# Feed-forward reordered around the first output sums, with the weight sums one place on and half of the next inputs split by GpSimd

## The chip, the cores and the metric

One program runs on one core of a Trainium2 chip. The metric is the device time of one execution in microseconds (us). A profiled execution gives the trace from which the rows below come; times in it count from the first instruction. The engines are named as the profile names them: PE (TensorE, matmuls), PEld (its weight loads), DVE (VectorE), ACT (ScalarE), POOL (GpSimd) and SP (the queue that issues DMAs). Each works through its own instructions strictly in the order in which the program lists them.

## What is computed

Attention with a mix of the heads before and after the softmax, then two feed-forward layers over 1792 tokens of width 768:

```python
x = attention(q, k, v, w_pre, w_post)          # 4 batches, 12 heads, 448 positions, head width 64
h = x @ w_in                                   # 768 -> 2048, layer 0
x = (h * np.cos(h)) @ w_out                    # 2048 -> 768
g, val = x @ w_gate, x @ w_val                 # 768 -> 1536 each, layer 1
out = (g / (1 + np.exp(-g)) * val) @ w_out2    # 1536 -> 768
```

## The kernel before

Attention runs first as a software pipeline. Its steps (`premix`, `rowmax`, `expo`, ...) are entered in a plan by block number; within a block the kinds of step are issued in the order of the table `ORDER`. The first weights of the feed-forward are prepared in attention's last blocks, as kinds of the same table (`w_max`, `w_sum`, `w_sum_all`, `w_unit`, `w_shift`, `w_bits`, `w_split`).

The feed-forward is written out by hand in `steps()`. It runs over pieces (layer, g, t): g is a group of 256 hidden units (8 groups in layer 0, 6 in layer 1), t one of four tiles of 448 tokens. Iteration i works on two pieces at once: the first matmuls and the nonlinearity of piece i, and the second matmuls of piece i-1.

- `l1` makes the hidden values of one half e (128 units): 18 matmuls (L718 to L720) into the PSUM tile `ph`, since each product is made of high and low halves of both operands. In layer 1 there are two columns (gate and value), so 36.
- `hidden` turns `ph` into `gh` (high half) and `gl` (low half). In layer 0: DVE makes `k` (L735) and `r` (L736), ACT takes the sine (L737), DVE multiplies (L739), ACT casts `gh` (L747), POOL subtracts for `gl` (L748). In layer 1: ACT does Silu (L745), DVE multiplies (L746), then the same.
- `l2` makes the six output sums m = 0 to 5 of the piece before, 6 matmuls each (L763 to L765), into the PSUM tile `py`, which has three buffers. Sum m is added to `acc` by DVE (L769), or, in the first group of a layer, copied there by ACT (L767). So the first matmul of the fourth sum (m = 3) must wait until the first sum has been taken out of its buffer, the fifth for the second, the sixth for the third.

Weights are converted between these steps. `fill(n)` issues the next n small steps of a list: one DVE instruction on a slab of weights (L514 maxima, L561, L563, L567 the bits), with the ACT and POOL instructions that belong to it (L553, L591, L592). When the maxima of a batch are complete, `sum_up` puts a tiny matmul `su` (L533) on PE, which spreads the maxima over the partitions, and two DVE instructions that read it (L541, L542); until then the batch's conversion is held back. The same matmul for activations is `sx` (L790, in `next_unit`). `su` and `sx` share one PSUM bank.

Between the layers the outputs of layer 0 become layer 1's inputs X[t], six parts m for each t, each split in a high and a low half: `next_hi` (ACT, L798) with `next_lo` (DVE, L812), or, for t = 0, `next_both` (ACT twice, L805 and L806, and POOL, L807). In the last group of layer 0 each sum's addition is followed by a maximum (L773).

The order inside one iteration before: fill; for each half e: three parts of the next inputs' high halves, `l1`, the whole of `hidden` (with one fill before its last multiply in layer 0), for e = 0 another fill, three parts of the low halves, `sum_up`; then the six sums of `l2`, with fills behind m = 1 and 3 (and 5 in layer 1 and the first iterations), then `sum_up`.

## Time and profile before

| | |
|---|---|
| three runs | 1433.23 us median (1430.79 to 1433.38) |
| the profiled execution, its own time | 1432.4 us |
| its span, first to last instruction | 1430.6 us |
| PE busy | 1393.1 us, 97% of the span |
| DVE busy | 1017.0 us, 71% |
| ACT busy | 615.7 us, 43% |
| POOL busy | 459.3 us, 32% |
| mean granted TensorE clock | 0.996 of full speed |
| DMA | 126.16 MB, mean 88 GB/s |

Matmuls are pipelined and one counts as busy until its end, so PE's busy share says little about small waits; they are read from the starts of the matmuls and from the view of waits. Attention fills the span to about 440 us and thins out until 465 us; layer 0 runs from there to about 960 us, layer 1 to the end.

### The profile page before, as it was taken

Reading aid. Unit: us, or ns where it says so; the run is one execution under the profiler, and the core shown is the slowest. Engines: PE = TensorE matmul, PEld = TensorE weight load, DVE = VectorE, ACT = ScalarE, POOL = GpSimd, SP = SyncE. Lnnn points to the kernel's source line nnn. Section 1 sums busy time; section 2 is a strip of 40 time slices with the busy share of each in tenths; the row PEclk is TensorE's granted clock in tenths of the full one; section 3 lists DMA queues with packets and bytes.
Section 4 is the critical chain, followed back from the end, with each engine's and each line's share of the span. In section 5 each row is a group of like instructions: output and inputs, shape, how many; then the busy total and the mean of one; then the engine's idle time right before and its main releaser. Section 6 shows DMA issues by size and latency. Waiting matters only on the chain.

```text
span 1430.6 us, 25097 instructions
## 1 busy us (share of the span) xinstructions
PE 1393.1 (97%) x9562; PEld 963.6 (67%) x9562; DVE 1017.0 (71%) x2166; ACT 615.7 (43%) x1310; POOL 459.3 (32%) x490
## 2 busy tenths in 40 slices
PE   6899999999999999999999999989999999999998
PEld 3577777767766666767676767656666666666666
DVE  5877887877888668888888888775456566565523
ACT  4676777677665543333333332544422222222210
POOL 2354453453323333333232332322222223222310
PEclk9999999999999999999999999999999999999999
DMA  5554554554556122221221121021211212120012
GB/s 178 148 154 126 162 156 124 157 159 129 150 157 211 55 56 67 67 67 55 58 76 56 56 78 45 23 66 45 67 45 45 67 53 81 45 66 24 1 43 112
DMA packets 100209, 126.16 MB, mean 88 GB/s; under 512 B 29592, under 2 KB 88440, under 8 KB 100088
## 3 DMA queue, kind: packets, MB, share of 16 engines
q1 hardware_dynamic: 99248, 123.26, 29.0%
q8 instruction: 75, 1.23, 0.4%
q10 hardware_dynamic: 840, 1.29, 0.3%
q14 instruction: 46, 0.38, 0.1%
HBM read 75.45 MB, written 10.37 MB: 60 GB/s over the span
## 4 chain that ended last, share of the span: by engine, by line
PE 78%; DVE 16%; ACT 3%; issue 2%; DMA 1%; POOL 0%; ACTq 0%; SPq 0%; DVEq 0%; POOLq 0%
PE ph L718 11%; PE ph L720 10%; PE ph L719 10%; PE psm L232 9%; PE py L763 8%; PE py L764 7%; PE py L765 7%; PE psv L306 5%; PE pss L207 4%; PE psa L281 2%; PE psa L282 2%; PE psa L283 2%; DVE r L736 2%; DVE acc L769 2%; DVE r L739 2%
## 5 line engine op out<-in xcount | busy, mean ns | idle before, releaser
L718 PE MATMUL ph<-x,h_i 128*128 128x448 f16 x960 | 338.9, 353 | 0.0
L719 PE MATMUL ph<-x,h_i 128*128 128x448 f16 x960 | 338.3, 352 | 0.0
L720 PE MATMUL ph<-x,l_i 128*128 128x448 f16 x960 | 338.3, 352 | 0.0
L763 PE MATMUL py<-gh,h_o 128*128 128x448 f32 x672 | 256.9, 382 | 12.8 <-ACT acc L767 6.3
L748 POOL TENSOR_TENSOR gl<-r,gh 128x448 fp32r<-128x448 f32 x112 | 131.8, 1177 | 404.8 <-ACT gh L747 395.8
L764 PE MATMUL py<-gl,h_o 128*128 128x448 f32 x672 | 244.6, 364 | 0.0
L765 PE MATMUL py<-gh,l_o 128*128 128x448 f32 x672 | 244.0, 363 | 0.0
L769 DVE TENSOR_TENSOR acc<-py,acc 128x448 f32<-128x448 f32 x288 | 174.3, 619 | 64.1 <-PE py L765 60.3
L261 POOL TENSOR_SCALAR eh<-e,sm 120x448 f16<-120x448 f32 x180 | 121.5, 675 | 247.5 <-DVE sm L256 160.3
L232 PE MATMUL psm<-x,wpre_sb 120*120 120x448 f32 x360 | 179.3, 581 | 5.6 <-ACT e L245 5.6
L718 PEld LDWEIGHTS <-h_i 128*128 128x128 f16 x960 | 93.8, 98 | 92.6 <-issue 10.3
L720 PEld LDWEIGHTS <-l_i 128*128 128x128 f16 x960 | 93.9, 98 | 87.7 <-POOL l_i L592 0.2
L245 ACT ACTIVATE e<-psm,sm 120x448 f32<-120x448 f32 x180 | 114.8, 638 | 87.5 <-DVE sm L237 79.6
L763 PEld LDWEIGHTS py<-gh,h_o 128*128 128x128 f32 x672 | 126.7, 188 | 38.3 <-DVE acc L769 15.9
L719 PEld LDWEIGHTS <-h_i 128*128 128x128 f16 x960 | 94.1, 98 | 82.2 <-issue 0.3
L237 DVE TENSOR_REDUCE sm<-psm 120x1 f32<-120x448 f32 x180 | 111.0, 617 | 40.3 <-PE psm L232 40.2
L746 DVE SCALAR_TENSOR_TENSOR r<-ph,by_i,r 128x448 f32<-128x448 f32 x48 | 32.8, 684 | 146.5 <-PE ph L720 117.8
L268 DVE SCALAR_TENSOR_TENSOR el<-e,sm,eh 120x448 f16<-120x448 f32 x180 | 136.1, 756 | 0.0
L592 POOL TENSOR_TENSOR l_i<-f_i,h_i 128x384 f16<-128x384 f32 x80 | 81.4, 1018 | 165.2 <-ACT h_i L591 165.1
L765 PEld LDWEIGHTS py<-gh,l_o 128*128 128x128 f32 x672 | 126.5, 188 | 9.0
L764 PEld LDWEIGHTS py<-gl,h_o 128*128 128x128 f32 x672 | 126.8, 189 | 7.4
L747 ACT CAST gh<-r 128x448 fp32r<-128x448 f32 x112 | 63.5, 567 | 155.6 <-DVE r L746 117.8
(103 smaller groups left out, 2284.8 us busy)
## 6 DMA issues: line engine op xcount, KB each, us to landing
r_o<-in_w_out SPq DMA_DIRECT2D x56, 384.0 KB
x<-s SPq DMA_DIRECT2D x84, 210.0 KB
r_i<-in_w_in SPq DMA_DIRECT2D x32, 384.0 KB
x<-s SPq DMA_DIRECT2D x48, 192.5 KB
r_i<-in_w_gate SPq DMA_DIRECT2D x24, 384.0 KB
r_i<-in_w_val SPq DMA_DIRECT2D x24, 384.0 KB
x<-s SPq DMA_DIRECT2D x48, 175.0 KB
qr<-in_qT SPq DMA_DIRECT2D x15, 360.0 KB
```

The costliest lines, as they stand in the source:

```text
L232: nc.tensor.matmul(ps[:120, :S], wpre_sb, X[b, c][:120, k], start=True, stop=True)
L245: nc.scalar.activation(e, PM.pop((b, c, k))[:120, :S], AF.Exp, bias=sm[:, 0:1], scale=1.0, accum_out=sm[:, 1:2])
L261: nc.gpsimd.tensor_scalar(eh, E[b, c, k], sm[:, 3:4], 1.0, op0=ALU.mult, op1=ALU.mult)
L268: nc.vector.scalar_tensor_tensor(el, E.pop((b, c, k)), sm[:, 3:4], eh, op0=ALU.mult, op1=ALU.subtract)
L718: nc.tensor.matmul(ps, wh, xh, start=(kk == 0), stop=False)
L719: nc.tensor.matmul(ps, wh, xl, start=False, stop=False)
L720: nc.tensor.matmul(ps, wl, xh, start=False, stop=(kk == 5))
L748: nc.gpsimd.tensor_tensor(gl, r, f(gh), op=ALU.subtract)
L763: nc.tensor.matmul(ps, wh, gh[:, e], start=(e == 0), stop=False)
L764: nc.tensor.matmul(ps, wh, gl[:, e], start=False, stop=False)
L765: nc.tensor.matmul(ps, wl, gh[:, e], start=False, stop=(e == 1))
L769: nc.vector.tensor_tensor(acc, ps, acc, op=ALU.add)
```

## The change

`hidden` is cut in two: `hidden_a` ends with the sine or the Silu, `hidden_b` holds the multiply, the cast and the subtraction. For the half e = 1, `hidden_b` is issued behind the first output sum (m = 0) with one fill ahead of it, no longer ahead of all six. The second `sum_up` of an iteration goes there too, and a `su` is issued one place later (tick - 2). The next inputs' parts 0 to 2 are issued behind the first half's `hidden_b`, parts 3 to 5 behind the sums m = 1 to 3; parts 3 to 5 of every t (not only of t = 0) are now split by ACT, ACT and POOL, where DVE made the low half. In layer 1's first two groups the scale factors (`w_by`) are made ahead of the fill. In `ORDER`, `w_sum_all`, `w_unit` and `w_shift` stand behind `premix`.

```diff
--- before.py
+++ after.py
@@ -36,8 +36,8 @@
 AT_DVE = (2, 5, 8)
 ORDER = (
     "scale_v", "mixed_out", "l1_part", "norm_hi", "dma_v", "spread", "post", "rowmax", "w_sum",
-    "w_sum_all", "w_unit", "w_bits", "hidden", "norm_lo", "den", "w_max", "w_shift", "w_split",
-    "expo", "lo_q", "dma_q", "lo_k", "qk", "rec", "premix", "pv_out", "hi_k", "dma_k", "w_dma",
+    "w_bits", "hidden", "norm_lo", "den", "w_max", "w_split", "expo", "lo_q", "dma_q", "lo_k", "qk",
+    "rec", "premix", "w_sum_all", "w_unit", "w_shift", "pv_out", "hi_k", "dma_k", "w_dma",
     "x_load", "load_next", "new_scale", "max_v", "pv", "hi_q",
 )
 SM = 1.0 / 8.0
@@ -666,7 +666,7 @@
     def sum_up(self, all=False):
 
         self.tick += not all
-        while self.sums and (all or self.sums[0][-1] < self.tick - 1):
+        while self.sums and (all or self.sums[0][-1] < self.tick - 2):
             *batch, _ = self.sums.pop(0)
             self.w_sum_all(batch)
             self.w_unit(batch)
@@ -719,31 +719,36 @@
         nc.tensor.matmul(ps, wh, xl, start=False, stop=False)
         nc.tensor.matmul(ps, wl, xh, start=False, stop=(kk == 5))
 
-    def hidden(self, layer, g, t, e, fill=0):
+    def hidden(self, layer, g, t, e):
+        self.hidden_a(layer, g, t, e)
+        self.hidden_b(layer, g, t, e)
+
+    def hidden_a(self, layer, g, t, e):
 
         nc = self.tc.nc
         if e == 0:
             self.G[g, t] = tuple(
                 self.p_g.tile([128, 2, S], F32R, tag=f"g{p}", name=f"g{p}{layer}_{g}_{t}") for p in "hl"
             )
-        gh, gl = (x[:, e] for x in self.G[g, t])
         r = self.p_t.tile([128, S], F32, tag="t", name=f"r{layer}_{g}_{t}_{e}")
+        self.part["r", t, e] = r
         if layer == 0:
             ps = self.PH[e, 0]
-            by, turn = (self.by[0, "i", 0, 2 * g + e][:, i, t:t + 1] for i in range(2))
+            turn = self.by[0, "i", 0, 2 * g + e][:, 1, t:t + 1]
             k = self.p_t.tile([128, S], I32, tag="t", name=f"k_{g}_{t}_{e}")
             nc.vector.tensor_scalar(k, ps, turn, 0.25, op0=ALU.mult, op1=ALU.add)
             nc.vector.scalar_tensor_tensor(r, ps, turn, k, op0=ALU.mult, op1=ALU.subtract)
             nc.scalar.activation(r, r, AF.Sin, bias=self.hpi, scale=TWOPI)
-            self.fill(fill)
-            nc.vector.scalar_tensor_tensor(r, ps, by, r, op0=ALU.mult, op1=ALU.mult)
         else:
-            if g < 2:
-                for col in range(2):
-                    self.w_by((1, "i", col, 2 * g + e), t)
-            by = [self.by[1, "i", col, 2 * g + e][:, 0, t:t + 1] for col in range(2)]
-            nc.scalar.activation(r, self.PH[e, 0], AF.Silu, scale=by[0])
-            nc.vector.scalar_tensor_tensor(r, self.PH[e, 1], by[1], r, op0=ALU.mult, op1=ALU.mult)
+            by = self.by[1, "i", 0, 2 * g + e][:, 0, t:t + 1]
+            nc.scalar.activation(r, self.PH[e, 0], AF.Silu, scale=by)
+
+    def hidden_b(self, layer, g, t, e):
+        nc = self.tc.nc
+        gh, gl = (x[:, e] for x in self.G[g, t])
+        r = self.part.pop(("r", t, e))
+        by = self.by[layer, "i", layer, 2 * g + e][:, 0, t:t + 1]
+        nc.vector.scalar_tensor_tensor(r, self.PH[e, layer], by, r, op0=ALU.mult, op1=ALU.mult)
         nc.scalar.copy(gh, r)
         nc.gpsimd.tensor_tensor(gl, r, f(gh), op=ALU.subtract)
 
@@ -793,25 +798,19 @@
         nc.vector.tensor_scalar(self.unit[1][:, t:t + 1], u, 2.0 ** -14, None, op0=ALU.mult)
         nc.vector.reciprocal(by, self.unit[1][:, t:t + 1])
 
-    def next_hi(self, t, ms):
-        for m in range(6)[ms]:
-            self.tc.nc.scalar.activation(self.X[t][0][:, m], self.acc[t][:, m], AF.Copy, scale=self.mx[t][:, 7:8])
-
...
+    def next_part(self, t, m):
+
+        nc = self.tc.nc
+        hi, lo = (x[:, m] for x in self.X[t])
+        by = self.mx[t][:, 7:8]
+        if t == 0 or m > 2:
             x = self.p_acc.tile([128, S], F32, tag="nx", bufs=2, name=f"nx_{t}_{m}")
-            nc.scalar.activation(x, self.acc[t][:, m], AF.Copy, scale=self.mx[t][:, 7:8])
+            nc.scalar.activation(x, self.acc[t][:, m], AF.Copy, scale=by)
             nc.scalar.copy(hi, x)
             nc.gpsimd.tensor_tensor(lo, x, hi, op=ALU.subtract)
-
...
+        else:
+            nc.scalar.activation(hi, self.acc[t][:, m], AF.Copy, scale=by)
+            nc.vector.scalar_tensor_tensor(lo, self.acc[t][:, m], by, hi, op0=ALU.mult, op1=ALU.subtract)
 
     def early_plan(self, s):
 
@@ -858,40 +857,51 @@
             self.now = i
             t_max = i - done - 2
             t_new = t_max - 1
+            L0, g0, t0 = seq[i - 1]
             if i > 1 and i < len(seq):
                 L, g, t = seq[i]
                 for batch in range(1 + L) if t == 0 else ():
                     self.need(("i", L, g, batch))
+                if L and g < 2:
+                    for e in range(2):
+                        for col in range(2):
+                            self.w_by((1, "i", col, 2 * g + e), t)
                 self.fill((3 + (i < 4), 5)[L])
                 shorten = 0 <= t_new < 4
-                for e in range(2):
-                    if shorten:
-                        (self.next_hi if t_new else self.next_both)(t_new, slice(3 * e, 3 * e + 3))
-                    if (i, e) != (2, 0):
-                        self.l1(L, g, t, e)
-                    self.hidden(L, g, t, e, 1)
-                    if e == 0:
-                        self.fill((1, 5)[L])
-                    if shorten and t_new:
-                        self.next_lo(t_new, slice(3 * e, 3 * e + 3))
-                    self.sum_up()
-            L, g, t = seq[i - 1]
-            if t == 0:
-                self.need(("o", L, g))
+                if i != 2:
+                    self.l1(L, g, t, 0)
+                self.hidden_a(L, g, t, 0)
+                self.fill(1)
+                self.hidden_b(L, g, t, 0)
+                self.fill((1, 5)[L])
+                if shorten:
+                    for m in range(3):
+                        self.next_part(t_new, m)
+                self.sum_up()
+                self.l1(L, g, t, 1)
+                self.hidden_a(L, g, t, 1)
+            if t0 == 0:
+                self.need(("o", L0, g0))
             if 0 <= t_max < 4:
                 self.next_max(t_max)
             if i == 1:
                 self.l1(0, 0, 2, 0)
             for m in range(6):
-                self.l2(L, g, t, m)
+                self.l2(L0, g0, t0, m)
                 if i == 1 and m == 0:
                     self.hidden(0, 0, 1, 1)
-                if m in (1, 3) or i == 1 or (m == 5 and (L or i < 4)):
+                if m == 0 and 1 < i < len(seq):
+                    self.fill(1)
+                    self.hidden_b(L, g, t, 1)
+                    self.sum_up()
+                if m in (1, 3) or i == 1 or (m == 5 and (L0 or i < 4)):
                     self.fill(1)
                 if 0 <= t_max < 4 and m == 3:
                     self.next_unit(t_max)
+                if 0 < m < 4 and 0 <= t_new < 4:
+                    self.next_part(t_new, m + 2)
             self.sum_up()
-            del self.G[g, t]
+            del self.G[g0, t0]
         assert not self.todo
```

DVE in layer 0, iteration of piece (0, 4, 1), around the start of the six sums of piece (0, 4, 0); `k` and `r0` belong to the half e = 1, `acc_01<-py0_4_0_m` takes out sum m. Before:

```order
L735 TENSOR_SCALAR k_4_1_1_9942<-ph0_4_1_1_0_9922,by_0_i_0_9_0_9442 128x448
L736 SCALAR_TENSOR_TENSOR r0_4_1_1_9941<-ph0_4_1_1_0_9922,by_0_i_0_9_0_9442,k_4_1_1_9942 128x448
L567 SCALAR_TENSOR_TENSOR f_0_i_0_11_1_9879<-r_0_i_0_11_1_9486,f_0_i_0_11_1_9879 128x384
L739 SCALAR_TENSOR_TENSOR r0_4_1_1_9941<-ph0_4_1_1_0_9922,by_0_i_0_9_0_9442,r0_4_1_1_9941 128x448
L769 TENSOR_TENSOR acc_01_7797<-py0_4_0_0_9954,acc_01_7797 128x448
L769 TENSOR_TENSOR acc_01_7797<-py0_4_0_1_9962,acc_01_7797 128x448
```

and with the change, where L774 is the addition and L751 the multiply:

```order
L739 TENSOR_SCALAR k_4_1_1_9947<-ph0_4_1_1_0_9927,by_0_i_0_9_0_9431 128x448
L740 SCALAR_TENSOR_TENSOR r0_4_1_1_9946<-ph0_4_1_1_0_9927,by_0_i_0_9_0_9431,k_4_1_1_9947 128x448
L774 TENSOR_TENSOR acc_01_7797<-py0_4_0_0_9951,acc_01_7797 128x448
L514 TENSOR_REDUCE u_0_i_0_12_0_9959<-r_0_i_0_12_0_9788 128x1
L751 SCALAR_TENSOR_TENSOR r0_4_1_1_9946<-ph0_4_1_1_0_9927,by_0_i_0_9_0_9431,r0_4_1_1_9946 128x448
L774 TENSOR_TENSOR acc_01_7797<-py0_4_0_1_9964,acc_01_7797 128x448
```

The first sum is taken out right behind `r0`; the fill and the multiply stand between the first and the second sum.

DVE again, between the layers, around the sums of piece (0, 7, 3); `x_12` are the low halves of X[1], `f_1_o` weights. Before:

```order
L812 SCALAR_TENSOR_TENSOR x_12_7213<-acc_01_7797,mx_1_11662,x_12_7213 128x448 x3
L602 TENSOR_SCALAR by_1_i_0_1_0_11986<-unit1_72,u_1_i_0_1_0_11330 128x1
L602 TENSOR_SCALAR by_1_i_1_1_0_11988<-unit1_72,u_1_i_0_1_0_11330 128x1
L746 SCALAR_TENSOR_TENSOR r1_0_0_1_11985<-ph1_0_0_1_1_11966,by_1_i_1_1_0_11988,r1_0_0_1_11985 128x448
L812 SCALAR_TENSOR_TENSOR x_12_7213<-acc_01_7797,mx_1_11662,x_12_7213 128x448 x3
L541 TENSOR_SCALAR u_1_i_0_2_0_11857<-su_1_i_0_2_0_11997 128x2
L542 TENSOR_SCALAR u_1_i_0_2_0_11857<-u_1_i_0_2_0_11857 128x2
L783 TENSOR_REDUCE mx_2_11804<-mx_2_11804 128x1
L769 TENSOR_TENSOR acc_3_7799<-py0_7_3_0_12002,acc_3_7799 128x448
```

and with the change:

```order
L813 SCALAR_TENSOR_TENSOR x_12_7213<-acc_01_7797,mx_1_11659,x_12_7213 128x448 x3
L788 TENSOR_REDUCE mx_2_11789<-mx_2_11789 128x1
L774 TENSOR_TENSOR acc_3_7799<-py0_7_3_0_11990,acc_3_7799 128x448
L778 TENSOR_REDUCE mx_3_11998<-acc_3_7799 128x1
L563 SCALAR_TENSOR_TENSOR f_1_o_0_1_11933<-r_1_o_0_1_11278,f_1_o_0_1_11933 128x384
L751 SCALAR_TENSOR_TENSOR r1_0_0_1_11987<-ph1_0_0_1_1_11968,by_1_i_1_1_0_11863,r1_0_0_1_11987 128x448
L774 TENSOR_TENSOR acc_3_7799<-py0_7_3_1_12006,acc_3_7799 128x448
```

Three of the six low halves are gone from DVE, and the multiply and the reading of `su` no longer stand ahead of the first sum.

ACT one iteration later, around the sums of piece (1, 0, 0), which ACT itself copies out (`acc_01<-py1_0_0_m`). Before:

```order
L798 ACTIVATE x_12_7213<-acc_2_7798,mx_2_11804 128x448 x3
L745 ACTIVATE r1_0_1_1_12195<-ph1_0_1_1_0_12157,by_1_i_0_1_0_11986 128x448
L747 CAST gh1_0_1_12123<-r1_0_1_1_12195 128x448
L767 COPY acc_01_7797<-py1_0_0_0_12206 128x448
L767 COPY acc_01_7797<-py1_0_0_1_12214 128x448
L767 COPY acc_01_7797<-py1_0_0_2_12223 128x448
```

and with the change, where L808 and L809 are the two ACT instructions of a part that POOL finishes:

```order
L744 ACTIVATE r1_0_1_1_12211<-ph1_0_1_1_0_12173,by_1_i_0_1_0_11861 128x448
L772 COPY acc_01_7797<-py1_0_0_0_12214 128x448
L752 CAST gh1_0_1_12140<-r1_0_1_1_12211 128x448
L772 COPY acc_01_7797<-py1_0_0_1_12226 128x448
L808 ACTIVATE nx_2_3_12235<-acc_2_7798,mx_2_11789 128x448
L809 CAST x_12_7213<-nx_2_3_12235 128x448
L772 COPY acc_01_7797<-py1_0_0_2_12239 128x448
```

The copy of the first sum has moved ahead of the cast of `gh`, and the parts 3 to 5 have moved in between the later copies.

## Rows read from the trace of the kernel before

**Rows 1.** Waits of the weight loads, stretches 526.4:880, 481:526.4, 880:960: who, total us, times, longest.

```profile
PEld py L763 <- DVE acc L769: 10.3, 27, 0.6
...
PEld py L763 <- ACT acc L767: 3.4, 3, 1.6
...
PEld py L763 <- DVE acc L769: 5.7, 4, 2.5
PEld py L763 <- ACT acc L767: 2.7, 1, 2.7
```

**Rows 2.** Busy time by stage: us, then PE, PEld, DVE, ACT, POOL, PEclk, DMA.

```profile
526.49:879.71 353.22, 351.12 (x1773) 249.44 (x1772) 296.25 (x551) 116.78 (x210) 112.08 (x105) 1.00 0.21 62
879.71:960.09 80.38, 73.45 (x366) 48.52 (x366) 66.67 (x134) 35.26 (x62) 25.39 (x22) 0.98 0.14 40
960.09:1412.26 452.17, 452.17 (x2351) 295.43 (x2350) 237.05 (x448) 121.86 (x226) 111.34 (x101) 1.00 0.17 50
```

**Rows 3.** Timeline of PE where blocks of matmuls begin: start, duration, instruction.

```profile
649.38 0.36 PE L718 MATMUL ph<-x,h_i 128*128 128x448 f16 x1
...
656.04 0.53 PE L763 MATMUL py<-gh,h_o 128*128 128x448 f32 x1
...
663.82 0.18 PE L533 MATMUL su_i<-u_i,ones 128*128 128x2 bf16 x1
663.86 0.35 PE L718 MATMUL ph<-x,h_i 128*128 128x448 f16 x1
...
1043.68 0.36 PE L718 MATMUL ph<-x,h_i 128*128 128x448 f16 x1
...
1064.64 0.36 PE L718 MATMUL ph<-x,h_i 128*128 128x448 f16 x1
...
1078.11 0.53 PE L763 MATMUL py<-gh,h_o 128*128 128x448 f32 x1
...
1085.48 0.36 PE L718 MATMUL ph<-x,h_i 128*128 128x448 f16 x1
```

**Rows 4.** Timeline of one step of layer 0, DVE, then ACT, then PEld.

```profile
657.20 0.68 DVE L736 SCALAR_TENSOR_TENSOR r<-ph,by_i,k 128x448 f32<-128x448 f32 x1
657.80 0.54 DVE L514 TENSOR_REDUCE u_i<-r_i 128x1 f32<-128x384 f32 x1
...
658.86 0.68 DVE L739 SCALAR_TENSOR_TENSOR r<-ph,by_i,r 128x448 f32<-128x448 f32 x1
659.45 1.14 DVE L769 TENSOR_TENSOR acc<-py,acc 128x448 f32<-128x448 f32 x2
...
657.98 0.67 ACT L737 ACTIVATE r<-r,hpi 128x448 f32<-128x448 f32 x1 [1.43 <-DVE r L736]
...
660.12 0.19 PEld L763 LDWEIGHTS py<-gh,h_o 128*128 128x128 f32 x1 [0.52 <-DVE acc L769]
```

**Rows 5.** Timeline between the layers, first long wait: ACT, DVE, PEld.

```profile
905.00 0.66 ACT L737 ACTIVATE r<-r,hpi 128x448 f32<-128x448 f32 x1
...
906.36 0.62 DVE L769 TENSOR_TENSOR acc<-py,acc 128x448 f32<-128x448 f32 x1
...
907.03 0.22 PEld L763 LDWEIGHTS py<-gh,h_o 128*128 128x128 f32 x1 [2.50 <-DVE acc L769]
```

**Rows 6.** Timeline between the layers, ahead of the second long wait: DVE, POOL.

```profile
928.52 2.75 DVE L812 SCALAR_TENSOR_TENSOR x<-acc,mx,x 128x448 f16<-128x448 f32 x3
...
929.28 1.51 POOL L748 TENSOR_TENSOR gl<-r,gh 128x448 fp32r<-128x448 f32 x1 [2.73 <-ACT gh L747]
```

**Rows 7.** Costliest groups of the page, one line: busy us, mean ns, idle before.

```profile
L748 POOL TENSOR_TENSOR gl<-r,gh 128x448 fp32r<-128x448 f32 x112 | 131.8, 1177 | 404.8 <-ACT gh L747 395.8
```

**Rows 8.** Timeline of PE in attention's last blocks.

```profile
429.58 0.16 PE L533 MATMUL su_i<-u_i,ones 128*128 128x2 bf16 x1 [2.35 <-DVE u_i L525]
```

**Rows 9.** Waits of DVE over the whole span.

```profile
DVE f_i L561 <- ACT f_i L553: 21.6, 21, 2.6
DVE f_o L561 <- ACT f_o L553: 11.8, 6, 5.0
```

More of the change, by code (lines that the diff above doesn't have):

```diff
@@ L794, in next_unit @@
         nc.vector.reciprocal(by, self.unit[1][:, t:t + 1])
-    def next_hi(self, t, ms):
-        for m in range(6)[ms]:
-            self.tc.nc.scalar.activation(self.X[t][0][:, m], self.acc[t][:, m], AF.Copy, scale=self.mx[t][:, 7:8])
-    def next_both(self, t, ms):
+    def next_part(self, t, m):
         nc = self.tc.nc
-        for m in range(6)[ms]:
-            hi, lo = (x[:, m] for x in self.X[t])
+        hi, lo = (x[:, m] for x in self.X[t])
+        by = self.mx[t][:, 7:8]
+        if t == 0 or m > 2:
             x = self.p_acc.tile([128, S], F32, tag="nx", bufs=2, name=f"nx_{t}_{m}")
-            nc.scalar.activation(x, self.acc[t][:, m], AF.Copy, scale=self.mx[t][:, 7:8])
+            nc.scalar.activation(x, self.acc[t][:, m], AF.Copy, scale=by)
             nc.scalar.copy(hi, x)
             nc.gpsimd.tensor_tensor(lo, x, hi, op=ALU.subtract)
-    def next_lo(self, t, ms):
-        for m in range(6)[ms]:
-            hi, lo = (x[:, m] for x in self.X[t])
-            self.tc.nc.vector.scalar_tensor_tensor(
-                lo, self.acc[t][:, m], self.mx[t][:, 7:8], hi, op0=ALU.mult, op1=ALU.subtract
-            )
+        else:
+            nc.scalar.activation(hi, self.acc[t][:, m], AF.Copy, scale=by)
+            nc.vector.scalar_tensor_tensor(lo, self.acc[t][:, m], by, hi, op0=ALU.mult, op1=ALU.subtract)
     def early_plan(self, s):
```

## Prediction

> **What bounds the kernel now.** I read the view of waits first, for the weight loads, since a load that waits holds every matmul behind it. In layer 0 all that matters there has one name: the first matmul of a sum waits for an earlier sum to be taken out of its buffer, 27 times for DVE in the steady part, 3 times for ACT in the first iterations, and 5 times, up to 2.7 us each, between the layers [rows 1]. The same view has no such wait after 960 us, where PE is busy in every microsecond of its stage [rows 2]. So layer 1 is at PE's own pace, and layer 0 is at PE's pace plus these waits.
>
> How much they cost I took from starts, not from the waits, which also count what a load normally idles. Six sums without a wait take 1085.48 - 1078.11 = 7.37 us, a layer 0 pair of first-matmul blocks 656.04 - 649.38 = 6.66 us, a layer 1 pair 1078.11 - 1064.64 = 13.47 us [rows 3]. The steady stage from 526.49 to 879.71 holds 25 blocks of sums and 24 pairs: 25 x 7.37 + 24 x 6.66 = 344.1 us of the 353.2 that it took [rows 2], so 9.1 us are lost; the seven `su` in it explain about 0.4, and 8.7 are waits. The stage between the layers holds four blocks of sums, two short and two long pairs: 29.5 + 13.3 + 26.9 = 69.7 of 80.4 us, so 10.7 lost, of which I give 0.6 to the `sx` and `su`; the 10.1 left is the waits of [rows 1] and a TensorE clock that was granted at 0.98 over the stage, a mean between its levels of 1.2 and 2.4 GHz [rows 2]. The first iterations lose some 3.2 of the 3.4 us that the waits show [rows 1].
>
> **Why the fourth sum waits.** One step shows it [rows 4]. The sums begin at 656.04 [rows 3], at 7.37 / 36 = 0.205 us a matmul; the fourth needs the first one's buffer at 656.04 + 18 x 0.205 = 659.73. DVE is done with `r` at 657.88, but then has a fill and the multiply ahead of the first addition, and the multiply waits for the sine. The addition starts at 659.45, and the load comes at 660.12 after 0.52 idle.
>
> **The change, part by part.**
>
> *Steady part of layer 0.* The first addition follows `r`: 657.88 + 0.57 (1.14 for two) = 658.45, 1.3 us before it is needed. What is late next is the second addition: fill 0.54, three tiny instructions of 0.5 in this step, and the multiply of 0.68, whose sine is over at 658.65, end at 660.2; the addition ends at 660.75, needed at 656.04 + 24 x 0.205 = 660.96. With a common fill there is 0.7 to spare, here 0.2. The later `gh` and `gl` are hidden by the next pair of 6.66 us, since the next iteration's sums read them. DVE goes from 296.3 / 353.2 = 84% to 86% and stays short of full [rows 2]. I leave 0.7 of the 8.7 for the steps whose fill is the slow one. **Gain 8.0; from 5 to 8.7.**
>
> *First iterations (481 to 526).* There ACT copies the sums out, behind the cast of `gh`, which waits for DVE's multiply. The copy now follows the sine. **Gain 2.9; from 1.5 to 3.2.**
>
> *Between the layers.* In the first long wait ACT had made three next-input parts ahead of the sine, which started at 905.00; the first addition came at 906.36 and the load waited 2.50 [rows 5]. Now that addition does not wait for the sine. The three parts still do, a little earlier: I put the sine at 904.3, so the multiply ends near 905.7 and the second addition near 906.3, while the fifth sum's turn comes 6 matmuls of 0.205 us behind the fourth's, whose load began to wait at 907.03 - 2.50 = 904.5, so near 905.9: 0.4 us late. In the second, three low halves took DVE 2.75 us right before the sums' additions [rows 6]; three of the six are gone, and the multiply with them. But each sum there costs DVE an addition and a maximum, the fill and the multiply come between the first and the second, and the `su` now behind the six sums must wait until DVE has read the `sx` out of their one bank: by the same counting the fifth and sixth sum are 0.65 late together, and the `su` 0.9. In the third ACT copies the first sum ahead of `gh`, but the second's copy is behind a multiply that is behind three low halves: 1.4 us. With 0.1 for the piece before, 3.6 stay of 10.1. **Gain 6.5; from 3 to 9.** The POOL and ACT work that is added, nine parts with one subtraction each and one more cast, lies in a stage where they are busy 25.4 and 35.3 of 80.4 us [rows 2]. By the same counting the last low half of X[1] is ready 0.8 us before the matmul that reads it, the tightest such place.
>
> *The weight sums.* Between a pair and its sums a `su` costs (1064.64 - 1043.68) - (1085.48 - 1064.64) = 0.12 us, between the sums and the next pair 0.04 [rows 3]. The change moves 14 from the first place to the second, and one into the middle of the sums, which I count as another 0.1. **Gain 1.0; from 0 to 1.3.** That they come one place later holds back conversions by about two fills of eight in an iteration; the list has some four to spare in a group of four iterations, so nothing is late.
>
> *Attention's weight sum.* PE waited 2.35 us for DVE there [rows 8]. `premix`, two matmuls, now fills a part of it, but the `su` behind it still waits for the same DVE instruction, and what PE does earlier hangs on DVE again a block later. I take a fifth of the wait, since only DVE's own idle time there can come back. **Gain 0.5; from -0.5 to 2.4.**
>
> *Layer 1.* 24 iterations without a wait; the second sum is then 0.9 us early by the same counting. **0; down to -2.**
>
> Sum: 8.0 + 2.9 + 6.5 + 1.0 + 0.5 = 18.9 us. The profiled execution took 1432.4 (span 1430.6), 0.8 below the median 1433.2. From the median: **1414 us**.
>
> **A rule that speaks against it.** While DVE made low halves, POOL's subtraction took 1.51 us [rows 6], against 1.18 in the mean [rows 7]: the two engines slow each other there by 0.33 us, and the forecast takes nothing for it, since half of the pairings go away with DVE's low halves. The Trainium skill ("SBUF — State Buffer", section "Who interferes with whom") goes further: a DVE instruction with two SBUF inputs and a GpSimd instruction that reads SBUF exclude each other for the whole instruction. By that, what POOL gains could hold DVE for its full length, which is the upper price of rival 2; the trace agrees in direction, and shows an overlap, not a full stop.
>
> **The rivals.**
>
> 1. *The wait moves to the fifth sum.* The fill and the multiply are the new work ahead of the second addition; the spare was worked out above as 0.2 to 0.7 us [rows 4]. For it: fills that wait on ACT, 33.4 us in all [rows 9]. Against: most of those lie ahead of the pair, and the spare holds a common fill. Half of the steady gain and a third of that between the layers would go: 18.9 - 4.0 - 2.2 = 12.7 us, **1421**.
> 2. *POOL against DVE between the layers.* Nine new subtractions each hold DVE for between 0.33 us and a whole subtraction of 1.18 [rows 6, 7], half of it where something waits: 1.5 to 5.3 us lost, in the middle 3.4, **1418**. Against: DVE has few instructions with two SBUF inputs among the sums.
> 3. *More is kept*: attention's full 2.4 and one more wait between the layers, **1410**.
> 4. *Slower.* The place is the one fill between the first and the second sum, in all 52 iterations. If it waits w for its ACT part, the second addition is w - 0.6 late (0.6 is the spare, taken near the common fill's). With mean w above 0.6 + 18.9 / 52 = 0.96 us the kernel is slower. All such waits of an iteration together are now 33.4 / 52 = 0.64 [rows 9]; they would have to gather at this one place and grow by half. At w = 1.2 it loses 52 x 0.6 = 31 and ends at **1445**.
> 5. *No effect:* DVE is so full that the order does not matter. It sits at 84% [rows 2], and its additions wait for PE in other places, so I give it little: **1432**.
>
> **How the numbers follow.** The forecast has 0.52 (1411 to 1417), rival 1 0.18, rival 2 0.11, rival 3 0.11, rival 4 0.05, rival 5 0.03. The range 1408 to 1423 takes in the first four; the sums of the lower bounds (9 us) and the upper (24.6) give 1424 and 1409. A change below 0.2%, 2.9 us, can't be told from none: faster 0.92, same 0.03, slower 0.05.
>
> **What would show it.** Right: in the waits of the weight loads of the steady part, nearly nothing left for DVE's additions, and an iteration of 14.05 us instead of 14.4; between the layers, waits at the fifth and sixth sum and one at a `su`, 3 to 4 us together; layer 1 unchanged, at 20.85 us an iteration. Wrong: the same waits under another sum's number, `k` or `r` of the next half starting late because DVE has fallen behind, a load that waits for POOL's low half of X, or an `l1` that waits for weights at the start of a group.

## The result and the profile after

The changed kernel takes 1418.45 us, the median of 5 runs (1416.49 to 1419.83), the kernel before 1433.15 (1430.79 to 1433.38): a ratio of 0.9901, interval 0.9887 to 0.9915. It is 14.7 us faster; 18.9 were forecast (1414, range 1408 to 1423).

The waits of the weight loads come first again; they answer to [rows 1]: the steady part (522.66 to 872.97 us), then the stretch between the layers (872.97 to 946.88). The columns are who waits for what, us in total, times, longest.

```profile
PEld py L768 <- DVE acc L774: 6.4, 10, 1.2
...
PEld py L768 <- DVE acc L774: 1.6, 2, 1.0
PEld py L768 <- ACT acc L772: 0.7, 2, 0.5
```

The 27 waits of the steady part have become 10, but the longest has doubled, from 0.6 to 1.2. Between the layers 8.4 us have become 2.3. The windows answer to [rows 2].

```profile
522.66:872.97 350.31, 346.68 (x1773) 250.87 (x1771) 288.14 (x552) 117.98 (x210) 114.08 (x106) 1.00 0.22 64
872.97:946.88 73.91, 71.34 (x366) 47.67 (x366) 63.60 (x137) 36.78 (x66) 29.14 (x28) 1.00 0.19 54
946.88:1398.34 451.46, 451.46 (x2351) 295.35 (x2350) 227.65 (x436) 124.24 (x232) 115.49 (x105) 1.00 0.16 49
```

The steady part is 2.9 us shorter (8.0 were forecast), the stretch between the layers 6.5, as forecast, and layer 1 0.7. For all runs below I cut the profiled execution at starts of matmul blocks on PE: the first sums; the fifth step's sums; the first pair between the layers; the sums behind the fifth pair from there; the last sums. Each row is one profiled execution, and the pieces, in us, lie between these cuts. The piece "between" is thus the stretch of [rows 2] with one pair of 13.5 us more. "Whole" runs from the first sums to the end (the piece of some 18.3 us behind the last sums is in it), and so leaves attention out. A piece that an edit leaves alone mostly agrees within 0.1 us, but not always: "layer 1" of the run with two fills is 0.7 longer.

```
kernel            first sums at   first it.   steady   between   layer 1   whole
before               468.16         58.33     353.22     94.04    438.51   962.43
after                467.42         55.24     350.31     87.38    437.99   949.25
e1_split_only        466.35         55.90     354.71     90.50    438.90   958.34
e2_shift_early       466.65         55.45     346.93     86.68    437.92   945.31
e3_fill_later        469.11         55.19     350.75     87.15    437.92   949.33
e4_dve_parts         466.95         55.46     350.22     90.51    437.99   952.51
e5_old_sums          467.51         55.97     354.76     87.13    438.90   955.08
e6_two_fills         466.87         55.74     346.32     87.38    438.63   946.84
e7_between           468.21         55.22     346.88     86.19    438.62   945.23
e8_all               468.07         55.44     345.33     86.01    439.17   944.28
e9_best              467.33         56.77     345.33     86.99    437.92   945.33
e10_sums_only        467.58         57.83     358.61     98.65    437.93   971.35
```

The parts of the gain, from the start of the first sums on through the row, are 0.74 + 3.09 + 2.91 + 6.66 + 0.52 = 13.9 us, the difference of the two spans.

Where are the 5 us that the steady part kept? By the starts, 15 of its 25 blocks of sums take 7.37 us, three with a weight sum behind them 7.41, and seven others lose: 1.4 at 522.66, 1.1 each at 552.10, 651.39 and 750.91, 0.4 at 850.22, 0.9 at 864.67, 0.2 at 722.63. That is 6.2 us in all, of which the forecast had left 1.1 (0.4 for the weight sums and 0.7). In five of the seven, 5.1 us together, the fifth sum waits for the second addition. One of these, DVE, then ACT, GpSimd and the weight loads:

```profile
552.64 0.17 DVE L524 TENSOR_SCALAR u_i<-u_i 128x2 f32<-128x2 f32 x1
552.85 1.08 DVE L525 TENSOR_SCALAR u_i<-u_i 128x2 int32<-128x2 int32 x1
553.84 0.67 DVE L739 TENSOR_SCALAR k<-ph,by_i 128x448 int32<-128x448 f32 x1
554.55 0.68 DVE L740 SCALAR_TENSOR_TENSOR r<-ph,by_i,k 128x448 f32<-128x448 f32 x1
555.15 0.61 DVE L774 TENSOR_TENSOR acc<-py,acc 128x448 f32<-128x448 f32 x1
556.47 0.36 DVE L561 TENSOR_SCALAR f_o<-f_o 128x384 int32<-128x384 int32 x1 [0.70 <-ACT f_o L553]
556.74 0.68 DVE L751 SCALAR_TENSOR_TENSOR r<-ph,by_i,r 128x448 f32<-128x448 f32 x1
557.34 0.61 DVE L774 TENSOR_TENSOR acc<-py,acc 128x448 f32<-128x448 f32 x1
...
555.33 0.67 ACT L741 ACTIVATE r<-r,hpi 128x448 f32<-128x448 f32 x1 [2.72 <-DVE r L740]
555.90 0.53 ACT L553 ACTIVATE f_o<-r_o 128x384 f32<-128x384 f32 x1
...
552.75 1.15 POOL L753 TENSOR_TENSOR gl<-r,gh 128x448 fp32r<-128x448 f32 x1 [4.49 <-ACT gh L752]
...
558.00 0.19 PEld L768 LDWEIGHTS py<-gh,h_o 128*128 128x128 f32 x1 [1.08 <-DVE acc L774]
```

The fifth sum's load waits 1.08 us for the second addition, at the place of rival 1. Two things make that addition late here. The fill between the sums is the first of a list of weights: the same fill issues ACT's shift, which stands behind the sine, and DVE waits 0.70 for it. And L525, on 128x2 elements, took 1.08 us instead of 0.17: it began 0.10 us behind GpSimd's subtraction and ended 0.03 behind the subtraction's end, as if DVE had been locked out until then. `k`, `r` and the sine behind it are 0.9 late.

The other two blocks have neither delay. At 864.67 the sixth sum waits 0.99 for the third addition, which stands behind the additions' maxima and a fill of 1.18 beside GpSimd; at 722.63 nothing waits, and the matmuls start 0.206 us apart where they otherwise start 0.200 apart.

```profile
868.68 0.61 DVE L774 TENSOR_TENSOR acc<-py,acc 128x448 f32<-128x448 f32 x1
869.33 0.62 DVE L778 TENSOR_REDUCE mx<-acc 128x1 f32<-128x448 f32 x1
869.86 1.18 DVE L561 TENSOR_SCALAR f_i<-f_i 128x384 int32<-128x384 int32 x1
870.96 0.62 DVE L774 TENSOR_TENSOR acc<-py,acc 128x448 f32<-128x448 f32 x1
...
871.63 0.19 PEld L768 LDWEIGHTS py<-gh,h_o 128*128 128x128 f32 x1 [0.99 <-DVE acc L774]
```

### The profile page after: what moved, and what is told of

Read it like the earlier page. It is cut to its first block, busy times and chain, and to the rows that moved or that the text cites. A ratio compares the mean times of both kernels' runs of the same rounds, so it can differ in the third digit from the quotient of the medians.

```text
span 1416.7 us, 25084 instructions
## 1 busy us (share of the span) xinstructions
PE 1385.8 (98%) x9562; PEld 964.0 (68%) x9562; DVE 993.4 (70%) x2157; ACT 621.0 (44%) x1319; POOL 469.5 (33%) x499
## 4 chain that ended last, share of the span: by engine, by line
PE 83%; DVE 9%; DMA 3%; ACT 2%; issue 2%; ACTq 1%; POOL 0%; SPq 0%; DVEq 0%; POOLq 0%
PE ph L718 12%; PE ph L720 12%; PE ph L719 12%; PE py L768 9%; PE py L769 8%; PE py L770 8%; PE psm L232 8%; PE psv L306 4%; PE pss L207 4%; PE psa L281 2%; PE psa L282 2%; PE psa L283 2%; DMA x<-s 2%; DVE el L268 1%; DVE sm L237 1%
## 5 line engine op out<-in xcount | busy, mean ns | idle before, releaser
L774 DVE TENSOR_TENSOR acc<-py,acc 128x448 f32<-128x448 f32 x288 | 177.5, 620 | 143.0 <-PE py L770 133.7
L753 POOL TENSOR_TENSOR gl<-r,gh 128x448 fp32r<-128x448 f32 x112 | 135.0, 1205 | 401.7 <-ACT gh L752 398.1
L751 DVE SCALAR_TENSOR_TENSOR r<-ph,by_i,r 128x448 f32<-128x448 f32 x112 | 76.3, 681 | 90.4 <-PE ph L720 73.6
L592 POOL TENSOR_TENSOR l_i<-f_i,h_i 128x384 f16<-128x384 f32 x80 | 78.1, 976 | 160.0 <-ACT h_i L591 160.0
```

Of the source, the lines that this page charges most:

```text
L753: nc.gpsimd.tensor_tensor(gl, r, f(gh), op=ALU.subtract)
L774: nc.vector.tensor_tensor(acc, ps, acc, op=ALU.add)
```

## The experiments

**Theory:** these two delays, the shift and the lock with GpSimd, are the 5.1 us; the cut of the feed-forward step brought the rest. **Rivals:** DVE's total work between the sums sets the time; the gain comes from the other parts of the change. Four runs first. Each ratio is to runs of the kernel before on the same chip.

**The cut alone**, on the kernel before:

```diff
-                    self.hidden(L, g, t, e, 1)
+                self.hidden_a(L, g, t, 1)
...
+                if m == 0 and 1 < i < len(seq):
+                    self.fill(1)
+                    self.hidden_b(L, g, t, 1)
+                    if shorten and t_new:
+                        self.next_lo(t_new, slice(3, 6))
+                    self.sum_up()
```

> The kernel before with one part of the change only: the feed-forward step is cut in two and its second half's multiply, cast and subtraction (with the fill, and the three low halves of the next inputs behind them) stand behind the first sum; next inputs, places of the weight sums and attention's order are as before. If the cut makes the gains of the first iterations and of the steady part, and about half of that between the layers: the first iterations gain 3.0 us, the steady part 2.5 to 3, between the layers 3 to 4, the start of the first sums stays at 468.2 us; about 1424. Rival, the next inputs' new split makes the gain between the layers: nothing is gained there, about 1427.5. Rival, the weight sums' later places matter for the steady part: it gains under 2 us.

Measured: 1426.97 us, ratio 0.9966 (0.9954 to 0.9979). The first iterations gain 2.4 (3.0 were expected) and the stretch between the layers 3.5, as expected, but the steady part is 1.5 us *longer* than before. My theory of the cut failed there, and the last rival, the places of the weight sums, held. The block at 550.82 takes 9.45 us; PE and DVE in it:

```profile
552.69 0.16 PE L533 MATMUL su_i<-u_i,ones 128*128 128x2 bf16 x1 [0.34 <-DVE u_i L525]
...
551.57 1.07 DVE L525 TENSOR_SCALAR u_i<-u_i 128x2 int32<-128x2 int32 x1
...
556.05 0.15 DVE L541 TENSOR_SCALAR u_i<-su_i 128x2 int32<-128x2 int32 x1
556.23 0.17 DVE L542 TENSOR_SCALAR u_i<-u_i 128x2 int32<-128x2 int32 x1
556.31 0.62 DVE L777 TENSOR_TENSOR acc<-py,acc 128x448 f32<-128x448 f32 x1
```

With the cut, the place where weight sums are made lies between the first and the second sum. There PE stops for the slow L525, and the sum's two readings stand ahead of the second addition.

**The shift one piece earlier:**

```diff
...
+                        *([(self.w_shift, *ahead)] if j == 3 and ahead else []),
...
-                    do = [(self.w_shift, key, z)] if j == k == 0 else []
+                    do = [(self.w_shift, key, z)] if j == k == 0 and not had else []
-                    if k == 1 and nxt:
-                        do.append((self.w_shift, *nxt))
+                    if k == 1 and soon:
+                        do.append((self.w_shift, *soon))
...
```

(`ahead` is the first key of the next list where its scale is known, `soon` the next key or that one.)

> The changed kernel with ACT's shift of the first weights of a list issued one piece earlier (with the last maximum, or two pieces ahead of the list's end), where the scale is known by then. If the blocks of sums that still lose 1.1 us do so because the fill between the first and the second sum is the first of a list, and its DVE instruction waits 0.58 to 0.76 us for a shift that stands behind the sine on ACT: that wait goes in all of them, the second addition comes 0.6 us earlier, the blocks of 8.46 to 8.75 us come down to 7.8 to 8.1, and the steady part gains 3 to 4.5 us, about 1414.5. Rival, the sine itself or DVE's three short instructions on the weight maxima (1.08 us for one of them at 552.85) set the time and the wait for the shift only stands in their place: the blocks stay within 0.2 us, about 1418.

Measured: 1413.95, ratio 0.987 (0.9855 to 0.9885); the steady part takes 346.9, 3.4 less. DVE, then ACT in the same block:

```profile
551.16 1.08 DVE L525 TENSOR_SCALAR u_i<-u_i 128x2 int32<-128x2 int32 x1
...
554.00 0.35 DVE L561 TENSOR_SCALAR f_o<-f_o 128x384 int32<-128x384 int32 x1
554.29 0.69 DVE L756 SCALAR_TENSOR_TENSOR r<-ph,by_i,r 128x448 f32<-128x448 f32 x1
...
550.83 0.54 ACT L553 ACTIVATE f_o<-r_o 128x384 f32<-128x384 f32 x1
```

The shift is done 2.6 us ahead and the wait is gone; the block takes 7.69. L525 still takes 1.08, and 0.3 us stay.

**The fill put behind the third sum:**

```diff
                 if m == 0 and 1 < i < len(seq):
-                    self.fill(1)
                     self.hidden_b(L, g, t, 1)
                     self.sum_up()
+                if m == 2 and 1 < i < len(seq):
+                    self.fill(1)
```

> The changed kernel with the fill between the first and the second sum put behind the third sum. If that fill is what makes the second addition late: the second addition follows the multiply, and the fifth sum is on time in every step. In the steps in which the fill is the first of a list its wait for ACT moves behind the second addition, and makes the third late by about 0.5 us: blocks of 7.37 to 7.9 us, a steady part shorter by 3 to 5 us, about 1414. Rival, the fill has one place as good as another because DVE's total work between the sums sets the pace: the same losses at the sixth sum, within 1 us of the changed kernel.

Measured: 1419.24, ratio 0.9905 (0.9892 to 0.9919), no gain. The first bad block is cured (7.38 at 524.30), but three keep 1.2 us (8.6 at 553.03), since the wait for the shift is now ahead of the third addition, by 0.55 us as expected; and other blocks, at 538.34, 638.46 and 738.76, lose 0.65 that lost nothing before. This place doesn't cure it; taking the wait away does.

**The next inputs' second halves by DVE:** `if t == 0 or m > 2:` becomes `if t == 0:`.

> The changed kernel with the second halves of the next inputs 1 to 3 again made by ACT and DVE alone (one cast and DVE's low half), not by two casts and GpSimd's subtraction. If GpSimd's nine subtractions hold DVE (rival 2 of the prediction): 1.5 to 5 us are gained between the layers, 1413.5 to 1417. If what counts is what DVE has to do between the sums' additions: each low half of 0.69 us stands ahead of an addition, the three blocks of sums between the layers grow by 0.7 to 2 us each, 1421 to 1424. Before 880 us and after 970 nothing differs.

Measured: 1420.32, ratio 0.9912 (0.9899 to 0.9926), between the layers 3.1 us more than with GpSimd: the second theory. (The intervals of this time and the changed kernel's overlap; the piece decides, since the others agree within 0.3.) The stretch from 915.51:

```profile
915.51:922.00 6.49, 6.47 (x33) 5.55 (x31) 5.76 (x10) 1.94 (x5) 1.15 (x1) 1.00 0.08 29
922.00:927.16 5.16, 1.51 (x7) 1.16 (x8) 4.24 (x9) 1.90 (x4) 1.01 (x1) 0.94 0.25 76
927.16:930.20 3.04, 3.04 (x10) 1.26 (x10) 2.90 (x8) 0.00 (x0) 0.00 (x0) 0.54 0.00 0
```

PE stands still for 3.6 of 5.2 us in two stops: for 2.4 the sixth sum waits for the third addition, which stands behind a low half that waits for its cast on ACT, and for 1.3 the `su` waits for DVE's reading. Then the TensorE clock is granted at 0.54 for 3 us, near its level of 1.2 GHz: the pair behind takes 14.82 instead of 13.47. So stops of 3.6 us were paid here with another 1.35.

Then I undid the two small parts, and took the causes away one by one.

**Weight sums at their old places:** `self.tick - 2` becomes `self.tick - 1`, and attention's order is the old one.

> The changed kernel with two parts undone: the weight sums again one place earlier, and attention's weight sum again ahead of the mix; the cut of the feed-forward step and the new split of the next inputs stay. If the later place is what made the cut pay in the steady part (with the cut alone that part took 354.7 us, with the whole change 350.3): the steady part is 354 to 355 us, with blocks of 9.4 us in which the weight sum stands between two sums and waits for the weight maximum; the part from the second sums of the feed-forward on loses 0.6 us more; between the layers no change (87.4 us); about 1423.5. Rival, the next inputs' split or the order of fills made the difference: 350.5 us, about 1419. The start of the first sums came at 466.4 and 468.2 us with the old order of attention's weight sum and at 466.7 to 469.1 with the new, so a gain of 0.5 there is expected to be lost in that spread.

Measured: 1423.64, ratio 0.9946 (0.9933 to 0.9959). The steady part takes 354.76 as with the cut alone, layer 1 0.9 more, the first iterations 0.7. So the later place is worth some 6 us once the step is cut: this kernel, 1423.64, lies just above the prediction's range. The first sums start at 466.35 to 468.16 in the four profiles with attention's old order, and at 466.65 to 469.11 in the eight with the new: means of 467.4 and 467.6, so nothing is seen of that part.

**Two fills ahead of the multiply:**

```diff
-                self.fill(1)
+                self.fill((2, 1)[L])
                 self.hidden_b(L, g, t, 0)
-                self.fill((1, 5)[L])
+                self.fill((0, 5)[L])
```

> The changed kernel with the two fills behind the first half's sine both put ahead of its multiply in layer 0 (one stood behind it). DVE's short work on the weight maxima then ends before GpSimd begins the subtraction of this half. If DVE's instruction of 0.17 us took 1.08 because GpSimd's subtraction began 0.1 us ahead of it, and these 0.9 us are one half of what makes the second addition late: the instruction takes 0.17, the four blocks of 7.8 to 8.5 us that have it come down to 7.4 to 7.7, and the steady part gains 2 to 3.5 us, about 1415.5. Rival, the wait for ACT's shift alone sets the second addition: the blocks stay above 8.2 us, within 1 us of the changed kernel.

Measured: 1414.92, ratio 0.9878 (0.9864 to 0.9891); the steady part takes 346.3, 4.0 less, and the four blocks are at 7.41. DVE, then GpSimd:

```profile
551.46 0.17 DVE L525 TENSOR_SCALAR u_i<-u_i 128x2 int32<-128x2 int32 x1
...
554.77 0.36 DVE L561 TENSOR_SCALAR f_o<-f_o 128x384 int32<-128x384 int32 x1 [0.71 <-ACT f_o L553]
...
553.01 1.16 POOL L753 TENSOR_TENSOR gl<-r,gh 128x448 fp32r<-128x448 f32 x1 [5.18 <-ACT gh L752]
```

L525 takes 0.17 again, and the wait for the shift, still 0.71, now costs nothing in these four (the block at 522.61 keeps 1.0). Each delay alone nearly fits into the spare; the two together did not. Neither run took work away from DVE but for the lock, so its total work is not the limit; in the changed kernel it is busy for 288.14 / 350.31 = 82% of the steady part, where the forecast had 86%.

**Between the layers**, on the kernel with the early shift:

```diff
+                if shorten and L:
+                    for m in range(3):
+                        self.next_part(t_new, m)
                 self.fill((1, 5)[L])
-                if shorten:
-                    for m in range(3):
-                        self.next_part(t_new, m)
...
                 self.hidden_a(L, g, t, 1)
+                if shorten and not L:
+                    for m in range(3):
+                        self.next_part(t_new, m)
...
-            self.sum_up()
+            self.sum_up(hold=0 <= t_max < 4)
```

> The kernel with the shift one piece early, and three changes between the layers: the first three parts of input 0 stand behind the sine of the second half, those of inputs 1 to 3 ahead of the five fills, and a weight sum due behind the sums of these steps goes one place on, so that it does not wait for the maximum's reading of the same bank. If the fifth sum there is late through a sine behind three pairs of ACT's casts, and the weight sum waits 1.1 us for DVE's reading: the blocks of 8.58 and 9.36 us come down to 7.5 to 7.7 and 7.8 to 8.3, the part between the layers (86.7 us with the early shift) takes 84 to 85, about 1411.8. Rival, DVE's additions with their maxima are the limit there: the block of 9.36 stays above 9, about 1413. Rival, input parts made later hold the next first sums: these pairs grow beyond 6.66 and 13.47 us.

Measured: 1414.27, ratio 0.9876 (0.9864 to 0.9889), 0.5 us between the layers. The causes were right: the block of 8.58 takes 7.50 and that of 9.36 8.09, while with the change one load waited for that sine and one weight sum for DVE, as these rows of the changed kernel show.

```profile
898.58 0.68 DVE L751 SCALAR_TENSOR_TENSOR r<-ph,by_i,r 128x448 f32<-128x448 f32 x1 [1.69 <-ACT r L741]
...
899.85 0.19 PEld L768 LDWEIGHTS py<-gh,h_o 128*128 128x128 f32 x1 [0.99 <-DVE acc L774]
...
925.18 0.16 PE L533 MATMUL su_i<-u_i,ones 128*128 128x2 bf16 x1 [1.10 <-DVE mx L796]
```

But the last rival held too: input 0's later parts make the next pair wait, 14.78 us instead of 13.47 (the pair after it takes 13.83); GpSimd's low half ends at 902.93 and the matmul that waits for it starts at 902.99.

```profile
901.90 1.03 POOL L815 TENSOR_TENSOR x<-nx,x 128x448 f16<-128x448 f32 x1 [0.38 <-ACT x L814]
...
902.99 0.35 PE L724 MATMUL ph<-x,h_i 128*128 128x448 f16 x1 [0.69 <-POOL x L815]
```

**All three together:**

> All three together: the shift one piece early, two fills ahead of the multiply, and the changes between the layers. If the three causes are apart, each leaves what it left alone: a steady part of 345.5 to 346.5 us (ideal 344.5 with the weight sums), 84 to 85 between the layers; about 1410.5. Rival, with the shift early the lock between DVE and GpSimd costs nothing more: the steady part stays at 346.9.

Measured: 1412.87, ratio 0.9864 (0.985 to 0.9879); 345.3 and 86.0 (the expected 84 to 85 was already missed by the run before). The steady part comes to just below what was expected, 5.0 less than in the changed kernel; that is less than 3.4 + 4.0, since both cures meet in the same blocks. Layer 1 loses 1.2: 0.7 in one block in which a sum waits for ACT's copy (8.03, and 8.10 in the run before), perhaps through the held weight sum, which is not shown, and 0.6 in three blocks without a wait whose matmuls start 0.206 us apart and not 0.200, as some do in the run with two fills, which holds no weight sum.

**Without the first sine's place and the hold:**

> The shift one piece early and two fills ahead of the multiply, as before, but between the layers only one change: the first three parts of the next inputs stand ahead of the fills behind the first half's multiply, not behind the second half's sine, and the weight sum keeps its place. If the run with all three lost between the layers because input 0's first parts came too late for the next first sums (their pair took 14.8 us instead of 13.47) and the held weight sums came to cost up to 0.7 us each in layer 1: the pair is 13.47 again, the block ahead of it 8.5, the weight sum waits 1.1 us again; steady part 345.3, between the layers 85.7 to 86.7, the rest 437.9; from the first sums on 1.5 to 2 us less than with all three, about 1411. Rival, the pair's growth has another cause: it stays near 14.8.

Measured: 1412.4, ratio 0.9856 (0.9841 to 0.9871), whole 945.3. The pair is 13.47 again and layer 1 at 437.9, but the block behind the first long pair stays at 9.35, so parts ahead of the fills alone bring nothing. The 1.5 to 2 us against all three did not come: the first block of sums took 11.3 us here instead of 9.7, with a granted clock of 0.58 in its last 4 us behind waits that the other runs have too; why only here, I did not settle.

```profile
474.60:478.60 4.00, 4.00 (x12) 3.40 (x13) 2.43 (x7) 1.25 (x3) 0.64 (x1) 0.58 0.00 0
```

Of the steady part's waits for DVE one is left, the sixth sum's in its last block:

```profile
PEld py L773 <- DVE acc L779: 1.0, 1, 1.0
```

The intervals of the early shift, all three and this one overlap: by their medians 4.5 to 6 us below the changed kernel, no better known.

**The later weight sums alone**, on the kernel before (`self.tick - 2`):

> The kernel before with one part of the change only: each weight sum one place later. If the later place pays only together with the cut (it clears the second addition's place of the sum's reading and of the wait for the weight maximum): before the cut no sum stood between two sums, so the steady part stays within 1 us of 353.2, the second part of the feed-forward step gains 0.5, about 1432. Rival, the later place is worth 4.4 us of the steady part by itself: 349 us there, about 1428.

Measured: 1440.82, ratio 1.0056 (1.0042 to 1.0069), *slower* by 7.8 us. Neither side was right: the steady part loses 5.4, the stretch between the layers 4.6. In the steady part the weight sum's readings now stand ahead of `k` (at 570.96 and 571.14, the second 0.94 long beside GpSimd), and the uncut step pays for it in its fourth sum. Between the layers one block takes 15.65 us:

```profile
909.50:915.30 5.80, 0.40 (x2) 0.03 (x1) 2.21 (x6) 4.95 (x10) 4.21 (x4) 0.87 0.00 0
915.30:920.80 5.50, 5.49 (x15) 4.60 (x16) 4.96 (x12) 1.07 (x3) 1.15 (x1) 0.51 0.00 0
```

PE stands still for 5.4 us, while ACT is busy for 4.95, 3.7 of them with next inputs ahead of the sine, and then runs 5.5 us at a granted clock of 0.51.

## Why the prediction was right, and where its parts were not

*Steady part: forecast 8.0, measured 2.9.* This is the term that was mis-sized, and it fell below its own bound of 5. The mechanism held, but only together with the weight sums' new place: most blocks take 7.37, and an iteration there 14.03, while the cut alone made the steady part 1.5 us longer. The step that failed is the spare of 0.2 to 0.7 us of the second addition. It took a common fill of 0.54 and three tiny instructions of 0.5 together; where the list begins, the fill costs 0.70 + 0.36, and the tiny ones 1.4. Rival 1 named the place and priced half the steady gain; 5.1 us of the 8 were lost there, and the prediction's first sign of being wrong, the same waits under another sum's number, is what the trace shows. Its "against", that most fills that wait for ACT lie ahead of the pair, did not help, because a handful at one place cost all of it. Early shift and moved fills, which take away one delay each, give 3.4 and 4.0 us of it back, and both 5.0.

*The rule on DVE and GpSimd.* The forecast took nothing for it, and looked for it only between the layers. The trace shows it in the steady part: 0.17 to 1.08 us for L525. The Trainium skill ("SBUF — State Buffer", section "Who interferes with whom") names `tensor_scalar` among the instructions that can take the ports shared with GpSimd, and calls these an exclusive lock, held for a whole instruction. The trace agrees: in all four slow cases L525 begins 0.1 us behind a subtraction and ends within 0.03 of its end. The prediction read "an overlap, not a full stop" out of a merged row; taken apart, the third low half in the kernel before was held too, 1.56 us instead of 0.68, 0.48 of them behind the end of the subtraction at 930.79.

```profile
929.72 1.56 DVE L812 SCALAR_TENSOR_TENSOR x<-acc,mx,x 128x448 f16<-128x448 f32 x1
```

As rival 2 had it, GpSimd's nine subtractions holding DVE, it is refuted in the net: GpSimd's parts are worth 3.1 us.

*Weight sums: forecast 1.0, measured some 6 in this kernel* (the first iterations, the steady part and layer 1 of the run with the old places), and a loss of 7.8 by themselves. I had costed what a `su` takes on PE, and not what DVE's readings hold up at the place. The cut alone gives 5 us, and loses in the steady part. So the gain belongs to neither: the cut makes the old place of the weight sum bad, and the cut makes the new one good. That both stood in one change was luck as far as the forecast goes.

*First iterations 2.9 (3.1), between the layers 6.5 (6.7), layer 1 0 (0.5 with its weight sums).* These held, down to the fifth sum and a `su` that waits (0.9 forecast, 1.1 measured); only the fifth sum was 1.0 late instead of 0.4 (the prediction's own counting gives 904.5 + 6 x 0.205 = 905.8 and not 905.9, so 0.5), because the sine ran at 897.88 behind all three of ACT's pairs. The cut and the next inputs' new split, with its new places, share that gain: 3.5 and, between the run with the cut alone and the one with the old sums, 90.50 - 87.13 = 3.4.

*Attention: 0.5.* Profiles with either order overlap; not shown to be anything.

The total came out in the range because three terms held, because the weight sums' new place, priced at 1.0 for another reason, kept the steady part from losing, and because the range was made to reach rival 1. The time, 1418.45, lies above the 1411 to 1417 that the forecast itself was given; it is rival 2's number, but by chance: what happened is rival 1, in the steady part alone, where it cost 5.1 us and not 4.0, while the 2.2 that it had priced between the layers were not lost. By the spans the sum was 5 us too high, and the one spare accounts for nearly all of that.

## What to carry over

A spare of a few tenths of a microsecond has to be priced with the worst instruction that can stand at that place, not the common one: here 5 blocks of 25 ate nearly two thirds of the steady gain. Parts of a reordering are not additive, since the cut alone gave 5.0 us, the later sums alone cost 7.8, and with the rest they gave 14.7; undo each before you credit it. A wait that was only moved, with the fill behind the third sum, was still there; the one that was taken away, by a shift issued a piece earlier, was not.

## What the hardware showed that I had not expected

I laid every DVE instruction of the changed kernel after 480 us over GpSimd's busy time. Those with only SBUF operands and more than one element a partition stretch: L525 takes 0.17 us in 13 cases without overlap and 0.90 in the mean of 5 with; L561 on `f_o` 0.36 and 0.68, L563 on it 0.55 and 0.92; L797, on one element, takes 0.15 in both. Those that read PSUM do not: L739 takes 0.68 in both, L774 0.62 in both; nor does the maximum L514, 0.54 in both.

After PE had stood still for 3.6 us in two stops, or for 5.4 in one, the clock was granted at 0.54 and 0.51 for 3 to 5.5 us (the level of 1.2 GHz), and once, in the run without the first sine's place and the hold, at 0.58 for 4 us behind stops of 1.8 us together. The changed kernel, whose longest wait between the layers is 1.1, keeps 1.00 there, where the kernel before had 0.98 [rows 2].
